# Decay tables of a retention + mixture-of-experts kernel: scans on VectorE in place of a table through DRAM

## The chip, the cores and the metric

The kernel runs on one core of a Trainium2 chip. The metric is the device time of one execution in microseconds (us). The engines are TensorE (PE in the profile, with its weight loads as PEld), VectorE (DVE), ScalarE (ACT), GpSimd (POOL), and SyncE (SP), which issues every DMA of this kernel from one queue.

## The reference

Three layers in a row on 1,536 tokens (2 sequences of 768) with 512 channels. What the change touches is the first, a retention layer with 8 heads of 64 channels and a decay `lam` per head:

```
Dmask   = lam ** (i - j)  for i >= j, else 0        # within a block
lam_pow = lam ** (i + 1)
for each block:
    out   = ((q k^T) * Dmask) v + (q * lam_pow) state
    state = lam ** block * state + (k * lam ** (block - 1 - j))^T v
```

The second layer is a mixture of 4 experts, `out += p[:, e] * (relu(x w1[e]) w2[e])` with `p = probs / (sum(probs) + 1e-9)`. The third is `g = silu(x w_in)`, `out = g w_out`. All data are float32 (the third layer's weights come as 64-bit words).

## The kernel before, in words

The retention layer works in blocks of 128 tokens: 12 units (`u = 2c + b`, block c of sequence b). A unit has four pieces, `prep` (on POOL, from block 1 on: `qs` = q times the query powers `qdec`, and `old` = decayed state), `scores` (on POOL `ks` = k times a column of `dmask`; on PE the products `s`; on DVE `a` = `s * dmask`), `mix` (on PE `xps`, then on ACT and DVE the two halves `xhi`, `xlo` of x) and `carry` (on PE `sps`, the new state). `dmask` holds for each partition and head one row of 128 powers of lam shifted by the partition; `qdec` holds 128 powers for each pair of heads.

Matrix products outside the retention layer split each float32 operand into a high and a low half: ACT makes the high half (L141), and DVE or POOL the low half (L142). Three products of halves replace one. The weights come in pairs of steps: one `u` transfer and one `d` transfer of 512 KB each, into two raw buffers of each kind; the next `u` or `d` is issued when the split of the one before has released its buffer. Weights 0 and 1 of phase "a" are split by DVE, all later ones by POOL.

Phase "a" (the experts) starts with group 0: 8 steps on the 256 tokens of block 0. Step i runs `gemm1(i)` (up, L470, output `ph`, whose high and low half are `hhi` on ACT and `hlo` on DVE, L480 and L481) and `gemm2(i - 2)` (down, L525, output `po`). `gemm1(i)` uses PSUM bank i mod 2, so it waits until `hlo` of step i - 2 has been made. The pieces of the later units are put between the steps: unit 2's `prep` at slot `PREP` (two slots a step), its `scores` after step 3, unit 3's `mix` after step 7. From step 4 on the kernel also loads 64-bit words of the third layer (`words`), halves their scale on ACT (L196) and decodes them on DVE.

The order is written out by hand and is the program's order on each engine: an instruction that waits holds everything behind it on the same engine. That holds for SP's queue too.

`powers()` makes the opening: it loads lam into one row a head, doubles powers by 7 small DVE multiplications, stores the table `zd` to DRAM, and reads it back as `dmask` (512 KB) and `qdec` (256 KB). `gates()` (9 DVE instructions on 12 partitions) normalizes the expert probabilities and stands between the table's making and the first `kv` load. `keep_warm(n)` issues n products of zeros on PE; one keep_warm call of n gives 2n matmul records.

Of the kernel before, what the change touches and what calls it, by code (L numbers as in the profile page):

```python
# [7 lines left out]
F32 = mybir.dt.float32  # L8
# [3 lines left out]
ALU = mybir.AluOpType  # L12
# [3 lines left out]
P = 128  # L16
B, H, S, D = 2, 8, 768, 64
NPAIR = H // 2
# [5 lines left out]
NF = 8  # L24
# [1 line left out]
TW = 512  # L26
HW = DM // 2
FIRST = 6
PREP = 1
NW = E * NF // 2  # L30
NV = NF

# [5 lines left out]
def kernel(  # L38
# [10 lines left out]
    nc = tc.nc  # L49

    def pool(stack, name, bufs=1, side="left", **kw):
        return stack.enter_context(tc.tile_pool(name=name, bufs=bufs, side=side, **kw))
# [10 lines left out]
    dram = pool(ctx, "dram", space=DRAM)  # L63
# [6 lines left out]
    acst = pool(att, "acst", side="right")  # L70
# [1 line left out]
    awk = pool(att, "awk", 2, side="right")  # L72
    w0p = pool(first, "w0p", 2, side="right")

    zd = dram.tile([H, 2 * P], F32, name="zd")
    pd = dram.tile([E, NT // P, P], F32, name="pd")
    wd = [dram.tile([P, 2, 2 * DM], F32, name=f"wd{i}") for i in range(NV)]

    dmask = acst.tile([P, NPAIR, 2, P], F32, name="dmask")
    qdec = acst.tile([P, NPAIR, P], F32, name="qdec")  # L80
    state = [acst.tile([P, NPAIR, D], F32, name=f"state{b}") for b in range(B)]
    zeros = acst.tile([P, NPAIR, P], F32, name="zeros")
# [15 lines left out]
    def load_qk(c, b):  # L98
        t = ald.tile([P, 2, NPAIR, P], F32, tag="qk", name="qkt")
        nc.sync.dma_start(out=t, in_=qk[c, b])  # L100
        qk_t[c, b] = t

    def load_kv(c, b, parts=(slice(0, 2),)):
        if (c, b) not in kv_t:
            kv_t[c, b] = ald.tile([P, 2, H, D], F32, tag="kv", name="kvt")
        for j in parts:
            nc.sync.dma_start(out=kv_t[c, b][:, j], in_=kv[c, b, :, j])
# [25 lines left out]
    def load(j, n=1):  # L133
        for _ in range(n):
            if nxt[j] < len(seq):
                ph, i, src = seq[nxt[j]]
                nxt[j] += 1
                (load_up, load_down)[j](src, i, (ph, i))

    def split(eng, hi, lo, src):  # L140
        nc.scalar.activation(out=hi, in_=src, func=AF.Copy)  # L141
        eng.tensor_tensor(out=lo, in0=src, in1=hi.bitcast(F32), op=ALU.subtract)  # L142
# [13 lines left out]
    def half_up(key, n, eng):  # L156
        hi, lo = up_t[key]
        s = slice(0, 4, 3) if n == 0 else slice(1, 3)
        split(eng, hi[:, s], lo[:, s], raw_t[key, 0][:, s])
        if n:  # L160
            load(0)

    def half_down(key, n, eng):
        hi, lo = down_t[key]
        split(eng, hi[:, n], lo[:, n], raw_t[key, 1][:, n])
        if n:
            load(1)

    def split_half(key, n, eng):

        half_up(key, n, eng)
        half_down(key, n, eng)
# [53 lines left out]
    def flush():  # L226
        while pending:
            pending.pop(0)()
# [21 lines left out]
    def decode_next(more):  # L250

        if jobs[0] < 4 * NV:
# [3 lines left out]
            pending.append(decode(jobs[0]))  # L256
            jobs[0] += 1

    def powers():
        z = acst.tile([H, 2 * P], F32, name="z")  # L260
        nc.sync.dma_start(out=z[:, P:P + 1], in_=lam)
        nc.vector.memset(z[:, :P - 1], 0.0)
        nc.vector.memset(z[:, P - 1:P], 1.0)
        load_probs()
        for b in range(B):
            load_qk(0, b)
        m = 1
        while m < P:
            o = P - 1 + m
            nc.vector.tensor_scalar_mul(z[:, o + 1:o + 1 + m], z[:, P:o + 1], z[:, o:o + 1])  # L270
            m *= 2
        nc.sync.dma_start(out=zd, in_=z)
        gates()
        for b in range(B):
            load_kv(0, b, [1])
        for m in range(2):
            nc.sync.dma_start(
                out=dmask[:, 2 * m:2 * m + 2],
                in_=bass.AP(
                    zd.tensor, zd.offset + m * H * P, [[1, P], [2 * P, NPAIR], [1, P]]  # L280
                ),
            )
        load(0)
        for b in range(B):
            load_kv(0, b, [0])
        for t in range(2):
            nc.sync.dma_start(
                out=qdec[t * D:(t + 1) * D],
                in_=bass.AP(
                    zd.tensor, zd.offset + t * 2 * P + P, [[0, D], [4 * P, NPAIR], [1, P]]  # L290
                ),
            )
        nc.gpsimd.memset(zeros, 0.0)
        keep_warm(3)

    def keep_warm(n):
        warm = psum.tile([P, NPAIR, P], F32, tag="po3", name="warm")
        for _ in range(n):
            nc.tensor.matmul(warm, lhsT=zeros[:, 0], rhs=zeros, start=True, stop=True)  # L299
# [3 lines left out]
    def gate_tile():  # L303
        return const.tile([P, 2 * TW], F32, tag="gate", name="gate", bufs=2)

    def load_probs():
        n = NT // P
        t = gate_tile().rearrange("p (e i) -> p e i", i=P)
        gate_t["probs"] = t[:n, :E], t[:n, E]
        nc.sync.dma_start(out=t[:n, :E], in_=probs)  # L310

    def gates():
        pt, sm = gate_t["probs"]
        nc.vector.tensor_tensor(out=sm, in0=pt[:, 0], in1=pt[:, 1], op=ALU.add)
        nc.vector.tensor_tensor(out=sm, in0=sm, in1=pt[:, 2], op=ALU.add)
        nc.vector.tensor_tensor(out=sm, in0=sm, in1=pt[:, 3], op=ALU.add)
        nc.vector.tensor_scalar_add(sm, sm, 1e-9)
        nc.vector.reciprocal(out=sm, in_=sm)
        for e in range(E):
            nc.vector.tensor_tensor(out=pt[:, e], in0=pt[:, e], in1=sm, op=ALU.mult)  # L320

    def store_gates():
        nc.sync.dma_start(out=pd.rearrange("e r i -> r e i"), in_=gate_t["probs"][0])
# [297 lines left out]
    fill = []  # L621
# [177 lines left out]

    with tc.manual_schedule():  # L800
        powers()
        load(1)
        load(0)
        load(1)
        for i in range(2):
            w_tiles(w0p, ("a", i))
        units = {b: attention(0, b) for b in range(B)}
# [1 line left out]
        def piece(u, j):  # L809
            if u not in units:  # L810
                units[u] = attention(u // B, u % B)
            units[u][j]()
# [2 lines left out]
        piece(1, 0)  # L815
        piece(0, 1)
        piece(1, 1)
        keep_warm(5)
        half_up(("a", 0), 0, nc.vector)
        piece(0, 2)  # L820
        piece(1, 2)
        for b in range(B):
            load_qk(1, b)
        half_up(("a", 0), 1, nc.vector)
        half_down(("a", 0), 0, nc.vector)
        half_down(("a", 0), 1, nc.vector)
        gemm1("a", 0)
        split_half(("a", 1), 0, nc.vector)
        piece(0, 3)
        piece(1, 3)  # L830
# [9 lines left out]
        def attend(slot):  # L840
            skip = FIRST if gi == 0 else 0
            if gi == 0 and slot == PREP:
                piece(2, 0)
# [6 lines left out]
        for i in range(na):  # L850
            gi, f = steps["a"][i]
            if f == 0:
                todo = plan.get(gi, [])
                if gi == 2:
                    first.close()
                elif gi == E:
                    flush()
                    store_decoded()
                    att.close()
                    tmp["comb"] = pool(ctx, "comb")  # L860
                    tmp["sums"] = pool(early, "sums", side="right")
                    mixing = combine(*x_raw)
            if i:
                gemm1("a", i)
            attend(2 * f)
            flush()
            if 2 <= i < na - 1:
                gemm2("a", i - 2)
            attend(2 * f + 1)
            if i == 3:  # L870
                store_gates()
            elif i == 5:
                load_gate("a", 0)
            elif i in (8, 18, 25):
                load_gate("a", {8: 1, 18: 2, 25: 3}[i])
            elif i == na - 4:
                load_gate("c", 0)
            if i == PREP + 3:
                start_decoder()
            elif PREP + 3 < i < 4 * NF and (i % 2 and i != 15 or i in (6, 10, 16, 18, 20)):  # L880
                decode_next(i < 4 * NF - 3)

            if i == 0:
                split_half(("a", 1), 1, nc.vector)
            elif i in (1, 3):
                w_tiles(wp, ("a", (i + 3) // 2))
                split_half(("a", (i + 3) // 2), 0, nc.gpsimd)
            elif i in (2, 4):
                split_half(("a", (i + 2) // 2), 1, nc.gpsimd)
            elif i >= 13 and i % 2:  # L890
                if i < na - 3:
                    split_up(("a", (i - 5) // 2))
                elif i == na - 3:
                    left_sums(("c", 0))
                else:
                    left_second(("c", 0))
                if 15 <= i < na - 1:
                    split_down(("a", (i - 7) // 2))
            elif i == na - 2:
                left_first(("c", 0))  # L900
            if gi == E:
                for job in mixing[f * 11 // NF:(f + 1) * 11 // NF]:
                    job()
# [131 lines left out]
```

## Time and profile before

| | |
|---|---|
| device time, median of 3 runs | 816.72 us (816.11 to 817.9) |
| profiled execution, span from first to last instruction | 814.1 us |
| median less that span | 2.6 us |
| PE busy | 807.5 us (99%) |
| DVE, ACT, POOL busy | 529.7, 326.4, 453.4 us (65%, 40%, 56%) |
| bytes moved | 95.93 MB, 118 GB/s on average |

The profiled execution's own time is given by its span; what lies around it is the difference to the median. Busy shares are averages over the whole span, and PE's record of being busy includes products of zeros and the pipelined ends of matmuls. So a change in the first 20 us can't be read from these shares; it is read from the order of time in the opening.

### The profile page before, as it was taken

To read this page: it belongs to the slowest core of one execution; us is meant where nothing else is said; L and a number is where in the kernel's file an instruction comes from. 1 tells how busy PE (TensorE), PEld (TensorE's weight loads), DVE (VectorE), ACT (ScalarE), POOL (GpSimd) and SP (SyncE) were. 2 spreads that over 40 slices of the span, in tenths; PEclk is the share of its full clock that TensorE was granted. 3 is DMA by queue.
4 is the path that set the end of the run, shared out by engine and by line. 5 is a ranking of instruction groups with operands and counts; after the bars stand their busy time and mean duration, and the time that the engine had idled before them with its cause. 6 is when DMAs were issued, how large, how long until landed. Compare 5 with 4: busy or idle time off the path is not lost.

```text
span 814.1 us, 11017 instructions
## 1 busy us (share of the span) xinstructions
PE 807.5 (99%) x4224; PEld 666.9 (82%) x4224; DVE 529.7 (65%) x762; ACT 326.4 (40%) x528; POOL 453.4 (56%) x333
## 2 busy tenths in 40 slices
PE   9999999999999999999999999999999999999998
PEld 5899877778888888888888888888888888888886
DVE  6375797545668588878888878865454345666666
ACT  3433332433446333333333333334454465444431
POOL 1824755525666666666666666754346666555631
PEclk9999999999999999999999999999999999999999
DMA  8885767533324223223322211122233131111002
GB/s 296 317 321 195 250 240 240 189 102 117 104 104 142 90 91 115 94 83 98 112 94 85 94 61 70 46 90 90 78 103 105 52 103 52 52 52 52 27 1 103
DMA packets 31434, 95.93 MB, mean 118 GB/s; under 512 B 3409, under 2 KB 5001, under 8 KB 31381
## 3 DMA queue, kind: packets, MB, share of 16 engines
q1 hardware_dynamic: 31380, 95.23, 35.1%
q8 instruction: 33, 0.54, 0.3%
q14 instruction: 21, 0.16, 0.1%
HBM read 83.65 MB, written 11.57 MB: 117 GB/s over the span
## 4 chain that ended last, share of the span: by engine, by line
PE 93%; DVE 3%; DMA 2%; issue 1%; ACT 1%; POOL 0%; SPq 0%; ACTq 0%; POOLq 0%
PE po L707 32%; PE po L525 14%; PE ph L470 14%; PE y L647 12%; PE x L647 8%; PE z L647 8%; PE warm L299 1%; PE s L374 1%; PE xps L401 1%; DMA words<-wts 1%; DMA u<-wts 1%; DVE dec L213 1%; DVE dec L209 1%; DVE tail L206 1%; PE xps L397 1%
## 5 line engine op out<-in xcount | busy, mean ns | idle before, releaser
L707 PE MATMUL po<-hlo,dh 128*128 128x512 f32 x384 | 149.6, 390 | 0.0
L707 PE MATMUL po<-hhi,dh 128*128 128x512 f32 x384 | 149.6, 390 | 0.0
L707 PE MATMUL po<-hhi,dl 128*128 128x512 f32 x384 | 149.6, 389 | 0.0
L719 DVE TENSOR_TENSOR acc<-po,acc 128x512 f32<-128x512 f32 x176 | 117.2, 683 | 43.2 <-PE po L707 43.2
L142 POOL TENSOR_TENSOR ub<-u,ua 128x256 fp32r<-128x256 f32 (+2 forms) x48 | 74.8, 1559 | 107.4 <-ACT ua L141 103.1
L142 POOL TENSOR_TENSOR dl<-d,dh 128x1024 fp32r<-128x1024 f32 (+1 forms) x48 | 114.3, 2380 | 28.8 <-ACT dh L141 28.8
L664 POOL TENSOR_TENSOR s<-s,s 128x512 f32<-128x512 f32 x48 | 63.2, 1319 | 50.3 <-ACT s L659 50.2
L142 POOL TENSOR_TENSOR uc<-u,uc 128x512 fp32r<-128x512 f32 x24 | 31.2, 1301 | 96.7 <-ACT uc L141 96.7
L707 PEld LDWEIGHTS po<-hhi,dl 128*128 128x128 f32 x384 | 72.1, 188 | 15.0
L707 PEld LDWEIGHTS po<-hhi,dh 128*128 128x128 f32 x384 | 72.1, 188 | 14.9
L707 PEld LDWEIGHTS po<-hlo,dh 128*128 128x128 f32 x384 | 72.1, 188 | 14.9
L497 ACT ACTIVATE hhi<-ph 128x512 fp32r<-128x512 f32 x40 | 23.9, 599 | 97.0 <-DVE ph L491 83.3
L142 POOL TENSOR_TENSOR ub<-us,ua 128x1024 fp32r<-128x1024 f32 x24 | 58.4, 2433 | 5.3 <-ACT ua L141 5.3
L525 PE MATMUL po<-hhi,dh 128*128 128x512 f32 (+1 forms) x224 | 58.7, 364 | 0.0
L525 PE MATMUL po<-hhi,dl 128*128 128x512 f32 (+1 forms) x224 | 57.7, 360 | 0.0
L525 PE MATMUL po<-hlo,dh 128*128 128x512 f32 (+1 forms) x224 | 57.6, 359 | 0.0
L470 PE MATMUL ph<-xhi,ua 128*128 128x512 f32 (+1 forms) x224 | 55.6, 371 | 1.2 <-DVE hlo L481 0.7
L141 ACT ACTIVATE dh<-d 128x1024 fp32r<-128x1024 f32 (+1 forms) x52 | 51.3, 988 | 9.2 <-POOL ub L142 2.6
L470 PE MATMUL ph<-xhi,ub 128*128 128x512 f32 (+1 forms) x224 | 53.1, 359 | 0.0
L470 PE MATMUL ph<-xlo,ua 128*128 128x512 f32 (+1 forms) x224 | 53.1, 359 | 0.0
L498 DVE TENSOR_TENSOR hlo<-ph,hhi 128x512 fp32r<-128x512 f32 x40 | 27.7, 692 | 27.8 <-ACT hhi L497 27.8
L470 PEld LDWEIGHTS ph<-xhi,ua 128*128 128x128 f32 x224 | 37.9, 189 | 9.4 <-DVE hlo L481 0.9
(128 smaller groups left out, 1577.7 us busy)
## 6 DMA issues: line engine op xcount, KB each, us to landing
u<-wts SPq DMA_DIRECT2D x32, 512.0 KB, 3.6
d<-wts SPq DMA_DIRECT2D x32, 512.0 KB, 3.7
words<-wts SPq DMA_DIRECT2D x32, 512.0 KB, 5.1
wd<-dec SPq DMA_DIRECT2D x32, 256.0 KB, 3.1
u<-wd SPq DMA_DIRECT2D x16, 512.0 KB, 3.7
d<-wd SPq DMA_DIRECT2D x16, 512.0 KB, 3.7
qkt<-qk SPq DMA_DIRECT2D x12, 512.0 KB, 5.9
kvt<-kv SPq DMA_DIRECT2D x10, 512.0 KB, 5.6
```

The costliest lines, as they stand in the source:

```text
L141: nc.scalar.activation(out=hi, in_=src, func=AF.Copy)
L142: eng.tensor_tensor(out=lo, in0=src, in1=hi.bitcast(F32), op=ALU.subtract)
L206: nc.vector.tensor_scalar(out=tail, in0=low, scalar1=2.0 ** -29, scalar2=None, op0=ALU.mult)
L209: nc.vector.scalar_tensor_tensor(out=f, in0=high, scalar=3, in1=f, op0=ALU.logical_shift_left, op1=ALU.bitwise_or,)
L470: nc.tensor.matmul(pt[:, :n], lhsT=w, rhs=x[:, k, o:o + n], start=(j == 0), stop=(j == len(ops) - 1),)
L497: nc.scalar.activation(out=hi, in_=pt, func=AF.Copy)
L498: nc.vector.tensor_tensor(out=lo, in0=pt, in1=hi.bitcast(F32), op=ALU.subtract)
L525: nc.tensor.matmul(po_t[d][:, :n], lhsT=w[:, d * P:(d + 1) * P], rhs=h[:, :n], start=(begin and j == 0), stop=(last and j == 2),)
L647: nc.tensor.matmul(to, lhsT=a[:, k * P:(k + 1) * P], rhs=b[:, k], start=(first and j == 0), stop=(j == len(ops) - 1), skip_group_check=not ...
L664: nc.gpsimd.tensor_tensor(out=t, in0=a, in1=b, op=ALU.add)
L707: nc.tensor.matmul(po, lhsT=w, rhs=h, start=(j == 0), stop=(j == len(ops) - 1))
L719: nc.vector.tensor_tensor(out=a, in0=po, in1=a, op=ALU.add)
```

## The change

`dmask` and `qdec` are made in place. lam is read twice from DRAM: as `lamall`, all 8 values on each of 128 partitions, and as `lamhalf`, 4 values on each partition (even heads on the lower 64, odd heads on the upper 64). On POOL an `affine_select` writes `unit`, a 128x128 tile with ones on an antidiagonal. On DVE 8 scans (`state = lam * state + unit`) write the rows of `dmask`, and 4 scans from 1.0 write `qdec`. The table `zd`, its store and its four reads go.

The opening's transfers are in a new order: lamall, q and k of sequence 0, v of sequence 0, q and k of sequence 1, v of sequence 1, the first `u` and `d`, the two lamhalf reads, both k-by-head halves, the second `u`, the probabilities; the second `d` comes after `mix` of unit 1. `gemm1(0)` stands ahead of the split of the first `d`. `mix` of unit 0 stands ahead of the first split of `u`. `keep_warm(3)` and `keep_warm(5)` become one `keep_warm(2)`. The query powers are made after step 1 (`query_powers`), the gates after step 2, and unit 2's `prep` moves from slot 1 to slot 5.

```
-PREP = 1
+PREP = 5
+DECODE = 4
...
+    def lam_scan(out, lam_col, add, initial):
+
+        nc.vector.tensor_tensor_scan(
+            out=out,
+            data0=lam_col.to_broadcast([P, P]),
+            data1=add,
+            initial=initial,
+            op0=ALU.mult,
+            op1=ALU.add,
+        )
+
     def powers():
-        z = acst.tile([H, 2 * P], F32, name="z")
-        nc.sync.dma_start(out=z[:, P:P + 1], in_=lam)
...
-        load_probs()
-        for b in range(B):
-            load_qk(0, b)
-        m = 1
-        while m < P:
-            o = P - 1 + m
-            nc.vector.tensor_scalar_mul(z[:, o + 1:o + 1 + m], z[:, P:o + 1], z[:, o:o + 1])
-            m *= 2
-        nc.sync.dma_start(out=zd, in_=z)
-        gates()
-        for b in range(B):
-            load_kv(0, b, [1])
-        for m in range(2):
-            nc.sync.dma_start(
-                out=dmask[:, 2 * m:2 * m + 2],
...
+        nc.sync.dma_start(
+            out=lam_t["all"], in_=bass.AP(lam.tensor, lam.offset, [[0, P], [1, H]])
+        )
+        nc.gpsimd.memset(zeros, 0.0)
+        unit_t = acst.tile([P, P], F32, name="unit")
+        nc.gpsimd.affine_select(
+            out=unit_t,
+            in_=zeros[:, 0],
...
+        keep_warm(2)
+        load_qk(0, 0)
+        load_kv(0, 0, [1])
+        load_qk(0, 1)
+        load_kv(0, 1, [1])
         load(0)
-        for b in range(B):
-            load_kv(0, b, [0])
+        load(1)
         for t in range(2):
             nc.sync.dma_start(
-                out=qdec[t * D:(t + 1) * D],
...
+                out=lam_t["half"][t * D:(t + 1) * D],
+                in_=bass.AP(lam.tensor, lam.offset + t, [[0, D], [2, NPAIR]]),
             )
-        nc.gpsimd.memset(zeros, 0.0)
-        keep_warm(3)
+        for h in range(H):
+            lam_scan(dmask[:, h // 2, h % 2], lam_t["all"][:, h:h + 1], unit_t, 0.0)
+
+    def query_powers():
+        for p in range(NPAIR):
+            lam_scan(qdec[:, p], lam_t["half"][:, p:p + 1], zeros[:, 0], 1.0)
...
         powers()
-        load(1)
+        for b in range(B):
+            load_kv(0, b, [0])
         load(0)
-        load(1)
+        load_probs()
...
         piece(1, 1)
-        keep_warm(5)
+        piece(0, 2)
         half_up(("a", 0), 0, nc.vector)
-        piece(0, 2)
         piece(1, 2)
+        load(1)
         for b in range(B):
             load_qk(1, b)
         half_up(("a", 0), 1, nc.vector)
+        gemm1("a", 0)
         half_down(("a", 0), 0, nc.vector)
         half_down(("a", 0), 1, nc.vector)
-        gemm1("a", 0)
...
-            if i == 3:
+            if i == 1:
+                query_powers()
+            elif i == 2:
+                gates()
+            elif i == 3:
                 store_gates()
```

## Rows read from the trace of the kernel before

**Rows 1.** The page: span, and the chain that ended last by engine.

```profile
span 814.1 us, 11017 instructions
...
PE 93%; DVE 3%; DMA 2%; issue 1%; ACT 1%; POOL 0%; SPq 0%; ACTq 0%; POOLq 0%
```

**Rows 2.** Waits of PE from 60 us to the end: total, times, longest.

```profile
PE sps L426 <- ACT xraw L412: 0.2, 1, 0.2
```

**Rows 3.** Timeline, PE, opening: start, us, instruction, idle before and its releaser.

```profile
1.31 5.49 PE L299 MATMUL warm<-zeros 128*128 128x512 f32 x6 [1.31 <-POOL zeros L293]
6.73 2.07 PE L374 MATMUL s<-qkt 64*128 64x128 f32 x32
8.73 4.56 PE L299 MATMUL warm<-zeros 128*128 128x512 f32 x10
13.22 1.97 PE L401 MATMUL xps<-a,kvt 128*64 128x128 f32 x32
15.67 0.78 PE L470 MATMUL ph<-xhi,ua 128*128 128x256 f32 x4 [0.48 <-ACT xhi L415]
...
17.33 1.15 PE L426 MATMUL sps<-kvt,ks 128*64 128x64 f32 x32
18.41 0.75 PE L470 MATMUL ph<-xhi,ua 128*128 128x256 f32 x4
...
23.73 0.74 PE L470 MATMUL ph<-xhi,ua 128*128 128x256 f32 x4 [0.74 <-DVE hlo L481]
```

**Rows 4.** Timeline, DVE and POOL, opening: start, us, instruction, idle before.

```profile
0.73 0.52 POOL L293 MEMSET zeros<- 128x512 f32 x1 [0.29 <-POOLq L1022]
...
2.09 1.76 DVE L270 TENSOR_SCALAR z<-z 8x1 f32<-8x1 f32 x7 [1.10 <-DMA z<-lam]
...
4.96 0.94 DVE L318 RECIPROCAL gate<-gate 12x128 f32<-12x128 f32 x1
...
5.93 0.88 DVE L320 TENSOR_TENSOR gate<-gate 12x128 f32<-12x128 f32 x4
...
10.42 2.74 DVE L382 TENSOR_TENSOR a<-s,dmask 128x256 f32<-128x256 f32 x8 [3.61 <-DMA dmask<-zd]
...
13.51 2.40 POOL L360 TENSOR_TENSOR ks<-kvt,dmask 128x512 f32<-128x512 f32 x2 [12.26 <-DMA kvt<-kv]
```

**Rows 5.** Windows: stretch, busy PE, PEld, DVE, ACT, POOL, clock, DMA share, GB/s.

```profile
0.00:5.00 5.00, 3.69 (x5) 1.63 (x6) 2.73 (x14) 1.28 (x1) 0.73 (x5) 1.00 0.46 157
5.00:10.00 5.00, 5.00 (x38) 2.78 (x37) 1.78 (x5) 0.00 (x0) 0.00 (x0) 1.00 0.78 266
...
20.00:25.00 5.00, 4.26 (x35) 4.05 (x35) 3.67 (x6) 1.55 (x4) 2.33 (x2) 1.00 1.03 410
...
32.00:35.00 3.00, 3.00 (x41) 2.63 (x38) 1.23 (x4) 2.07 (x6) 3.00 (x4) 1.00 0.81 195
```

**Rows 6.** Timeline, all engines: from the third u transfer to unit 3's mix.

```profile
17.16 0.33 SPq L115 DMA_DIRECT2D u<-wts  x1
...
20.46 1.30 POOL L344 TENSOR_TENSOR qs<-qkt,qdec 128x512 f32<-128x512 f32 x1 [4.55 <-DMA qkt<-qk]
...
21.71 1.08 POOL L348 TENSOR_TENSOR old<-state,qdec 128x256 f32<-128x256 f32 x1
...
24.52 0.63 ACT L141 ACTIVATE ua<-u 128x512 fp32r<-128x512 f32 x1 [3.45 <-DMA u<-wts]
...
29.00 1.30 POOL L142 TENSOR_TENSOR dl<-d,dh 128x512 fp32r<-128x512 f32 x1
...
31.61 0.96 SPq L233 DMA_DIRECT2D words<-wts  x2
...
39.97 0.69 ACT L196 ACTIVATE words<-words 128x512 f32<-128x512 f32 x1 [4.66 <-DMA words<-wts]
...
42.63 0.66 PE L397 MATMUL xps<-qs,state 64*64 64x128 f32 x14 [0.17 <-DVE a L382]
```

**Rows 7.** Tile qkt up to 60 us: its transfers, from issue to landing.

```profile
DMA to landing us min/median/max: 3.7/6.3/9.8
```

More of the change, by code (lines that the diff above doesn't have):

```diff
@@ L73 @@
     w0p = pool(first, "w0p", 2, side="right")
-    zd = dram.tile([H, 2 * P], F32, name="zd")
     pd = dram.tile([E, NT // P, P], F32, name="pd")
@@ L257, in decode_next @@
             jobs[0] += 1
-    def powers():
-        z = acst.tile([H, 2 * P], F32, name="z")
-        nc.sync.dma_start(out=z[:, P:P + 1], in_=lam)
-        nc.vector.memset(z[:, :P - 1], 0.0)
-        nc.vector.memset(z[:, P - 1:P], 1.0)
-        load_probs()
-        for b in range(B):
-            load_qk(0, b)
-        m = 1
-        while m < P:
-            o = P - 1 + m
-            nc.vector.tensor_scalar_mul(z[:, o + 1:o + 1 + m], z[:, P:o + 1], z[:, o:o + 1])
-            m *= 2
-        nc.sync.dma_start(out=zd, in_=z)
-        gates()
-        for b in range(B):
-            load_kv(0, b, [1])
-        for m in range(2):
-            nc.sync.dma_start(
-                out=dmask[:, 2 * m:2 * m + 2],
[L279 to L282, printed above, removed]
+    lam_t = {}
@@ new lines, in lam_scan @@
+    def lam_scan(out, lam_col, add, initial):
[7 more added lines that the diff above has]
+        )
+    def powers():
+        lam_t["all"] = acst.tile([P, H], F32, name="lamall")
+        lam_t["half"] = acst.tile([P, NPAIR], F32, name="lamhalf")
+        nc.sync.dma_start(
[6 more added lines that the diff above has]
+            in_=zeros[:, 0],
+            pattern=[[1, P]],
+            base=1 - P,
+            channel_multiplier=1,
+            compare_op=ALU.not_equal,
+            fill=1.0,
+        )
+        keep_warm(2)
[3 more added lines that the diff above has]
+        load_kv(0, 1, [1])
@@ L283, in powers @@
         load(0)
-        for b in range(B):
-            load_kv(0, b, [0])
+        load(1)
         for t in range(2):
             nc.sync.dma_start(
-                out=qdec[t * D:(t + 1) * D],
-                in_=bass.AP(
-                    zd.tensor, zd.offset + t * 2 * P + P, [[0, D], [4 * P, NPAIR], [1, P]]
-                ),
-            )
-        nc.gpsimd.memset(zeros, 0.0)
-        keep_warm(3)
+                out=lam_t["half"][t * D:(t + 1) * D],
+                in_=bass.AP(lam.tensor, lam.offset + t, [[0, D], [2, NPAIR]]),
+            )
@@ L877 @@
                 load_gate("c", 0)
-            if i == PREP + 3:
+            if i == DECODE:
                 start_decoder()
-            elif PREP + 3 < i < 4 * NF and (i % 2 and i != 15 or i in (6, 10, 16, 18, 20)):
+            elif DECODE < i < 4 * NF and (i % 2 and i != 15 or i in (6, 10, 16, 18, 20)):
                 decode_next(i < 4 * NF - 3)
```

## The prediction

> **What bounds the kernel now.** I read the page first: the chain that ended last lies on PE for 93% of the span of 814.1 us [rows 1]. Then the waits of PE: from 60 us on PE waited 0.2 us in all [rows 2]. So PE's stream is dense from there to the end, and the change can give or take time only by making that dense stream begin earlier or later. All that counts is in the first 45 us, so I read those in order of time.
>
> In the opening PE issues products of zeros, 16 records of them, and real work of only about 4 us, until `gemm1(0)` starts at 15.67 us [rows 3]. What is late there is the mask: DVE stands idle for 3.61 us until `dmask` lands at 10.42 [rows 4], which has gone from lam to a table, to DRAM, and back. The windows say what this costs the transfers: the DMA engines are 46% busy in the first 5 us and 78% in the next 5, then full (1.03, at 410 GB/s in 20 to 25 us) [rows 5]. About 3.8 us of DMA time is lost (0.54 x 5 + 0.22 x 5), because SP's queue stood behind the table.
>
> The last tight place is at 42.63: unit 3's `mix` waits 0.17 us for `a` [rows 6]. Behind it is a chain through many engines. The third `u` lands at 24.52; ACT and POOL split this weight pair until 30.30 (29.00 + 1.30); this frees the raw buffers, SP issues the fifth `u` and `d` and then, at 31.61, the first `words`; these land at 39.97, and ACT, which is in order, has been waiting for them for 4.66 us with `hhi` of step 6 behind. `hlo`, `a` and `mix` follow [rows 6]. So there are two paths to the dense stream, PE's own and that of `words`, and before they arrive within 0.2 us of each other. The gain is the smaller of what the two paths gain.
>
> **Transfers.** The first big one is issued near 1.2 us (engines start at 0.73 [rows 4], one issue takes 0.48, half of the 0.96 for two [rows 6]). The quickest load of q and k took 3.7 us to land [rows 7], so 4.9. From there the queue never runs dry. At 410 GB/s [rows 5] 512 KB (524,288 bytes) take 1.28 us and half of it 0.64: v of sequence 0 at 5.5, q and k of sequence 1 at 6.8, its v at 7.5, the first `u` at 8.7, the first `d` at 10.0. The two lamhalf reads are 512 pieces of 4 bytes, which no row shows. Between nothing and the price of two 512 KB transfers, 2.6 us, I take 0.7, nearer to the lower end, since they carry only 2 KB. Then the k halves at 11.4 and 12.0, the second `u` at 13.3, the second `d` at 14.6, block 1's q and k at 17.2, the third `u` at 18.5.
>
> **Mask.** The single lamall read should land as the lam read did, by 2.1 to 2.6 [rows 4]. `affine_select` follows the memset (done at 1.25); it costs between nothing and POOL's 1.30 us for a pass four times as wide [rows 6], so it is done by 2.6 and hidden behind lamall. A scan over 128 columns stands in no row. The lower bound is 0.22 us (a 12x128 product, 0.88 for four), the upper 0.94 (the reciprocal, DVE's dearest row of 128 columns); I take 0.34, the 128x256 product (2.74 for eight) [rows 4], for a scan's element must wait for the one before it. Eight are 2.7 us: `dmask` is there at 5.3, with 4.4 and 10.1 as bounds.
>
> [...]
>
> **PE's own path.** One unit's `scores` take 1.03 us and its `xps` 0.98 (halves of 2.07 and 1.97) [rows 3], four mask products 1.37. Unit 0: `scores` 4.9 to 6.0, `a` to 7.4. Unit 1: `scores` 6.8 to 7.9, `a` to 9.3. `xps` of unit 0 from 7.9 to 8.9, of unit 1 from 9.4 to 10.4; ACT's `xhi` some 0.8 later. `gemm1(0)` at 11.2 against 15.67; its weights (8.7, and two splits of 0.7) are there. The zeros of keep_warm(2) end before 4.9 (4 of the 6 records that now take 5.49). Now the k halves, which move behind more transfers, are late: `ks` takes 1.2 us a unit [rows 4] from 11.4, so 13.8, and the two `carry` pieces stand in PE's order ahead of `gemm1(1)`: 14.5 against 18.41. From there to `gemm1(3)` PE now takes 5.32 us, of which 0.74 is a wait for `hlo` behind DVE's splits [rows 3]. With `gemm1(0)` ahead of the splits, and no POOL work beside them, I find that `hlo` ready at 18.9 in DVE's order, so `gemm1(3)` at 19.1 against 23.73. PE's path gains 4.6 us.
>
> **The words path.** The third `u` is issued once the first is split, near 12.4 (two splits behind unit 1's `a`), and lands at 18.5 by bytes; the same transfer now needs 7.3 us behind a full queue (17.16 to 24.52 [rows 6]), which would be 19.7. I take 19.1; the upper bound is 21.3, if the split is done only at 14. From there to the `words` issue it now takes 7.09 us (24.52 to 31.61). Unit 2's `prep` comes on top. Now POOL does it before the third `u` is there (20.46 to 22.79), for nothing; in slot 5 it stands between the two halves of this split, and its 1.30 + 1.08 = 2.38 us count in full [rows 6]. `words` at 19.1 + 7.09 + 2.38 = 28.57 against 31.61: 3.0 us. If they land as slowly as now, `mix` of unit 3 moves by 3.0.
>
> **Moved at no cost.** The gates (2.96 us, from the table's end at 3.85 to 6.81 [rows 4]) go to DVE after step 2, about 20.6 to 23.6. Behind them wait `hlo` of step 3, wanted by `gemm1(5)` near 28, and `a` of unit 2, wanted by its `mix` near 26: done by 25.3, so 0.8 us to spare. The query powers, 4 x 0.34 = 1.4 us, delay `hlo` of step 2 to 20.6, wanted at 23.5. Without that cover they would cost 3.0 and 1.4, but on PE's path, which has 1.6 us more than the words path. The probabilities (24 KB) and their store stay ahead of their use. The removed `zd` traffic (0.77 MB, 1.9 us at 410 GB/s) is already in the list of landings.
>
> **Sum.** The smaller gain decides: 3.0 us. Span 814.1 - 3.0 = 811.1; the median lies 2.6 us above that span, so 816.7 - 3.0 = 813.7 us. A measurement here tells about 0.2% (1.6 us) from no change.
>
> **Rivals.**
> *PE's path alone decides* (15%). In 32 to 35 us the DMA engines moved only 195 GB/s at a share of 0.81 [rows 5], less than half of the 410 of other stretches. If `words` then come about 2 us sooner after their issue, the words path gains 5 and PE's 4.6 rules: 812.1. Against it: nothing in the change touches that stretch.
> *The supply eats it: no change* (19%). The third `u` lands at 21.3, or POOL is slowed by DVE's scans and gates beside its splits; each us there takes one off. At 21.3 the gain is 31.61 - 30.77 = 0.8: 815.9. Scans of 0.94 lead to the same place: `dmask` at 10.1 is as late as the table was (10.42), and the change would not do what it says. For it: the DMA engines are full in 20 to 25 us as it is [rows 5], and unit 2's `prep` is a new charge on POOL.
> *PE runs at its low clock: slower* (9%). [...]
>
> [...]
>
> **Chances.** The forecast 57% (812.6 to 815.0), PE's path alone 15%, no change 19%, slower 9%. Faster by over 0.2% (below 815.1): 0.72; within: 0.19; slower: 0.09. The range for 8 in 10 takes in PE's path alone and the no-change case to its end: 811.9 to 816.6.
>
> **What would show it.** `a` of unit 0 starts near 6 instead of 10.42, after eight scans of about 0.34 us. `gemm1(0)` starts near 11.2, then PE waits for `ks`; `gemm1(1)` at 14.5, `gemm1(3)` at 19.1 without a wait for `hlo`. `qs` of unit 2 stands between two splits. `words` are issued near 28.6, and `mix` of unit 3 waits some 1.7 us for `a`, the difference of the two paths. PE's waits from 60 us on stay near 0.2. The prediction is wrong if `dmask` comes after 9, if records of one shape are spaced twofold beyond 10 us, or if `words` move by another amount than PE's stream at 45 us.

## The result: slower by 0.8%

The changed kernel takes 823.12 us (median of 4 runs, 821.26 to 824.51), the kernel before beside it 816.41 us (815.83 to 817.9): a ratio of 1.0077, 95% interval 1.0058 to 1.0095. The forecast was 813.7 with a range of 811.9 to 816.6. The span of the profiled execution grows from 814.1 [rows 1] to 821.7 us. PE waits for nothing from 60 us on (0.2 us in all before [rows 2]), so the loss lies in the first 60 us.

PE's timeline of the changed kernel (start, us, instruction, idle before and its releaser), to be read against [rows 3, 6]:

```profile
5.43 1.16 PE L386 MATMUL s<-qkt 64*128 64x128 f32 x16 [0.39 <-DMA qkt<-qk]
7.80 1.68 PE L386 MATMUL s<-qkt 64*128 64x128 f32 x16 [1.21 <-DMA qkt<-qk]
...
12.96 0.78 PE L482 MATMUL ph<-xhi,ua 128*128 128x256 f32 x4 [0.49 <-ACT xhi L427]
...
17.31 0.69 PE L438 MATMUL sps<-kvt,ks 128*64 128x64 f32 x16 [2.63 <-POOL ks L372]
18.77 1.12 PE L438 MATMUL sps<-kvt,ks 128*64 128x64 f32 x16 [0.78 <-POOL ks L372]
19.82 1.22 PE L482 MATMUL ph<-xhi,ua 128*128 128x256 f32 x4
...
25.12 0.63 PE L482 MATMUL ph<-xhi,ua 128*128 128x256 f32 x4
...
30.66 0.62 PE L537 MATMUL po<-hhi,dh 128*128 128x256 f32 x4
...
36.70 1.63 PE L409 MATMUL xps<-qs,state 64*64 64x128 f32 x16 [4.51 <-DVE a L394]
38.26 1.98 PE L413 MATMUL xps<-a,kvt 128*64 128x128 f32 x16
40.16 1.22 PE L482 MATMUL ph<-xhi,ua 128*128 128x256 f32 x4
...
42.78 0.69 PE L438 MATMUL sps<-kvt,ks 128*64 128x64 f32 x16
```

`gemm1(0)` does start earlier (12.96 against 15.67). Then PE waits 2.63 and 0.78 us for `ks`, and `gemm1(1)`, at 19.82, is already 1.4 us later than before. The great loss is at 36.70: `mix` of unit 2 waits 4.51 us for `a`, and the products behind it run at about half the rate (`xps` 3.46 us instead of 1.62).

DVE's timeline of the changed kernel shows, in its first rows, the scans and the `a` of unit 0, and then what the `a` of unit 2 waits behind (its own start is the last row):

```profile
3.65 2.63 DVE L263 TENSOR_TENSOR_SCAN dmask<-lamall,unit 128x128 f32<-128x128 f32 x8 [3.65 <-DMA lamall<-lam]
6.63 1.42 DVE L394 TENSOR_TENSOR a<-s,dmask 128x256 f32<-128x256 f32 x4 [0.35 <-PE s L386]
...
26.67 0.88 DVE L326 TENSOR_TENSOR gate<-gate 12x128 f32<-12x128 f32 x1
27.58 1.25 DVE L327 TENSOR_TENSOR gate<-gate 12x128 f32<-12x128 f32 x1
28.86 0.59 DVE L328 TENSOR_TENSOR gate<-gate 12x128 f32<-12x128 f32 x1
29.49 1.20 DVE L329 TENSOR_SCALAR gate<-gate 12x128 f32<-12x128 f32 x1
30.73 0.94 DVE L330 RECIPROCAL gate<-gate 12x128 f32<-12x128 f32 x1
31.71 3.91 DVE L332 TENSOR_TENSOR gate<-gate 12x128 f32<-12x128 f32 x4
35.55 0.41 DVE L493 SCALAR_TENSOR_TENSOR hlo<-ph,hhi 128x256 fp32r<-128x256 f32 x1
35.88 1.27 DVE L394 TENSOR_TENSOR a<-s,dmask 128x512 f32<-128x512 f32 x2
```

The nine gate instructions run from 26.67 to 35.62: 8.95 us, where they took 2.96 in the opening [rows 4]. Four products that took 0.88 take 3.91. The reciprocal keeps its 0.94, and `hlo` and `a`, which have one of their operands in PSUM, take 0.41 and 1.27 (0.42 and 1.28 in the kernel before). POOL works from 24.84 us to past the end of the gates without a pause (splits of weights, `qs`, `old`, `ks`).

Windows of the changed kernel (columns as in [rows 5]): the DMA engines, full from 5 to 10 us (share 1.02), fall to 0.21 from 10.5 to 14 us; and from 36 to 40 us the granted clock is 0.50.

```profile
10.50:14.00 3.50, 3.01 (x34) 2.77 (x31) 2.55 (x8) 2.27 (x6) 0.00 (x0) 0.83 0.21 64
36.00:40.00 4.00, 3.30 (x32) 2.58 (x32) 1.48 (x3) 0.00 (x0) 1.33 (x2) 0.50 0.94 342
```

SP was not late: lamhalf's two reads were issued from 4.33 us on, and the k halves, the second `u`, the probabilities and the second `d` were all issued behind them before the hole begins. What stood next in the queue is lamhalf. SP's row, and the time that the tile's view gives the two reads to land:

```profile
4.33 1.39 SPq L297 DMA_DIRECT2D lamhalf<-lam  x2
...
DMA to landing us min/median/max: 7.7/8.9/10.0
```

POOL's timeline has the first k half behind them, at 15.89 where the forecast had 11.4:

```profile
15.89 2.82 POOL L372 TENSOR_TENSOR ks<-kvt,dmask 128x512 f32<-128x512 f32 x2 [14.27 <-DMA kvt<-kv]
```

The same places of PE's timeline in the kernel before:

```profile
29.42 0.64 PE L525 MATMUL po<-hhi,dh 128*128 128x256 f32 x4
...
30.95 0.67 PE L397 MATMUL xps<-qs,state 64*64 64x128 f32 x16
...
32.57 0.75 PE L470 MATMUL ph<-xhi,ua 128*128 128x256 f32 x4
...
34.20 0.69 PE L426 MATMUL sps<-kvt,ks 128*64 128x64 f32 x16
```

Worked out along PE's order: `gemm2(2)` stands 1.24 us later than before (30.66 against 29.42 at its start); the wait adds 4.51; `xps` of unit 2 takes 3.46 instead of 1.62 us (36.70 to 40.16, against 30.95 to 32.57), 1.84 more; `gemm1(5)` 2.62 instead of 1.63, 0.99 more. That is 8.58 us at the `carry` of unit 2 (42.78 against 34.20). About 0.6 comes back at `mix` of unit 3, which no longer waits, and some 0.4 in small pieces after it, whose place was not followed: 7.6 in the span.

### The profile page after: what moved, and what is told of

Same layout as the page of the kernel before. It is cut to its first block, busy times and chain, and to the rows that moved or that the text cites. A ratio compares the mean times of both kernels' runs of the same rounds, so it can differ in the third digit from the quotient of the medians.

```text
span 821.7 us, 10996 instructions
## 1 busy us (share of the span) xinstructions
PE 806.4 (98%) x4212; PEld 668.6 (81%) x4212; DVE 527.5 (64%) x765; ACT 326.3 (40%) x528; POOL 459.5 (56%) x334
## 4 chain that ended last, share of the span: by engine, by line
PE 96%; DMA 2%; DVE 2%; ACT 0%; SPq 0%; issue 0%
PE po L719 32%; PE ph L482 16%; PE po L537 16%; PE y L659 12%; PE x L659 8%; PE z L659 8%; PE xps L413 2%; PE s L386 1%; DMA d<-wts 1%; PE xps L409 1%; DMA qkt<-qk 1%; PE sps L438 1%; DVE gate L332 0%; DVE dl L142 0%; DVE gate L327 0%; DVE gate L329 0%
## 5 line engine op out<-in xcount | busy, mean ns | idle before, releaser
L676 POOL TENSOR_TENSOR s<-s,s 128x512 f32<-128x512 f32 x48 | 68.9, 1437 | 44.7 <-ACT s L671 44.6
```

The lines of the kernel that those rows point to most:

```text
L676: nc.gpsimd.tensor_tensor(out=t, in0=a, in1=b, op=ALU.add)
```

## The experiments

Theory A: two things went wrong that the prediction had priced too low, the gates beside POOL's work and the 4-byte reads; the low clock follows from the waits. Theory B: the low clock of PE, for want of products of zeros, is the cause by itself. Theory C: the gates are hidden behind other work and cost nothing. Each ratio is to the kernel before, run beside it.

**Gates back in the opening** (between the mask products and `mix` of unit 0, probabilities loaded first):

```
-        load_probs()                     # behind the second u
+        load_probs()                     # behind lamall
...
         piece(1, 1)
+        gates()
         piece(0, 2)
...
-            elif i == 2:
-                gates()
```

> The changed kernel, with the probabilities loaded behind lamall and the gates made on DVE between the mask products of unit 1 and the mix of unit 0, where POOL stands idle. Theory A (gates in step 2 take 8.9 us because POOL's splits hold them up, and hold the mask product of unit 2): the gates take about 3.0 us, mix of unit 2 no longer waits 4.5 us, and the 2.8 us that its xps and the gemm1 behind it lose at the low clock come back: about 6 us less than the changed kernel's 823.1, near 817. Theory B (the low clock for want of products of zeros is the cause by itself): the gates get quick but xps and gemm1 of 36 to 42 us stay spaced twofold, and no more than 3 to 4 us come back, near 819.5. Theory C (the gates are hidden): no change, 823.

817.96 us, ratio 1.0020 (1.0010 to 1.0029). The gates take 3.04 us there (10.71 to 13.75), `mix` of unit 2 waits for nothing, and its products run at the rate of the kernel before (32.91 to 34.53, 1.62 us). 5.2 us came back. C falls. B falls as the cause at 36 us: no products of zeros were added, and the low clock there is gone with the wait (granted clock 1.00 from 30 to 40 us). The opening still has one: behind waits of 1.68 and 0.78 us for `ks`, `gemm1` of steps 1 and 2 takes 4.47 us (20.03 to 24.50) against 2.98 before, at a granted clock of 0.66 from 20 to 25 us.

**lamhalf copied on DVE from lamall:**

```
-        for t in range(2):
-            nc.sync.dma_start(out=lam_t["half"][t * D:(t + 1) * D], ...)
...
     def query_powers():
+        for t in range(2):
+            r = slice(t * D, (t + 1) * D)
+            nc.vector.tensor_copy(lam_t["half"][r],
+                lam_t["all"].rearrange("p (j t) -> p j t", t=2)[r, :, t])
```

> The changed kernel without the two lamhalf reads: lamhalf is copied on DVE from lamall, two copies of 64x4 ahead of the query powers. Theory A (1,024 bytes in pieces of 4 bytes stop the DMA engines for some 4 us at 10 to 14 us, so that the k halves land at 15.8): the k halves land near 11.5, gemm1 of step 1 starts near 15 to 16 instead of 19.8, the DMA share of 10 to 15 us rises from 0.38 to about 1.0, and the time falls by 3.5 to 4.5 us, near 819, the wait of mix of unit 2 for the gates staying near 4.5 us. Rival (the engines run dry because SP issues late, behind waits of its own): the share of 10 to 15 us stays low and the time within 1 us of 823.

819.07 us, ratio 1.0032 (1.0023 to 1.0042): 4.1 less. The DMA share of 10 to 15 us is 1.03 (0.38 in the changed kernel):

```profile
10.00:15.00 5.00, 4.14 (x56) 3.41 (x56) 4.04 (x10) 3.42 (x9) 2.53 (x2) 1.00 1.03 398
```

PE's timeline is near the predicted one: `gemm1` of step 0 at 12.17, of step 1 at 15.31, of step 3 at 19.66 (forecast 11.2, 14.5, 19.1). The wait for `a` stays, 6.1 us. So the 4-byte reads were most of the difference between the forecast opening and the measured one: at `gemm1` of step 3, 5.5 us of 6.0 (25.12 against 19.66 and 19.1).

**Both:**

> Both edits together. Theory A: the two causes add up, 10 us less than the changed kernel, near 813 to 814.5, below the kernel before (816.4); what is left is the words path, with mix of unit 3 waiting 1 to 2 us. Theory B (clock): PE's clock still falls in the gaps of the opening and the time stays at 816 or above.

818.01 us, ratio 1.0013 (1.0000 to 1.0027): a miss. With the k halves early, POOL makes `ks` at 12.50, and there the gates' four products meet it. DVE's timeline:

```profile
12.68 2.49 DVE L333 TENSOR_TENSOR gate<-gate 12x128 f32<-12x128 f32 x4
15.10 0.74 DVE L429 TENSOR_TENSOR xlo<-xps,xhi 128x256 fp32r<-128x256 f32 x2
```

2.49 us instead of 0.88, the same loss in another place. `xlo` and the first splits come later, `gemm1(0)` waits 3.84 us for `xlo`, and the third `u` is issued at 17.72 (13.75 with the copies alone).

**Gates in step 2, their sum in PSUM:**

```
         pt, sm = gate_t["probs"]
+        sm = bank([P, TW], "sm")[:NT // P, :P]
```

> The changed kernel with the gates in step 2 as they are, but their running sum in a PSUM bank, so that eight of the nine instructions have at most one operand in SBUF besides their output. If what holds them up beside POOL is two SBUF operands on DVE (the mask products and hlo, which read PSUM, keep their 0.64 and 0.42 us in the same stretch), the gates take 3 to 4 us instead of 8.9 and the time falls as in the first kernel, near 817 to 818. If POOL's splits hold up anything on DVE that writes or reads SBUF there, they stay near 8 us and the time near 823.

820.27 us, ratio 1.0044 (1.0030 to 1.0059). In the same place, with POOL splitting from 25.16 us on without a pause, the first gate, whose two operands both lie in SBUF, takes 0.86 us, and the sums and products with the running sum in PSUM 0.29 and 0.87, what they take beside an idle POOL (0.28 and 0.89 in the first experiment). DVE's timeline:

```profile
27.01 0.86 DVE L327 TENSOR_TENSOR sm<-gate 12x128 f32<-12x128 f32 x1
27.91 0.29 DVE L328 TENSOR_TENSOR sm<-sm,gate 12x128 f32<-12x128 f32 x1
28.23 0.29 DVE L329 TENSOR_TENSOR sm<-sm,gate 12x128 f32<-12x128 f32 x1
28.55 0.29 DVE L330 TENSOR_SCALAR sm<-sm 12x128 f32<-12x128 f32 x1
28.87 0.95 DVE L331 RECIPROCAL sm<-sm 12x128 f32<-12x128 f32 x1
29.86 0.87 DVE L333 TENSOR_TENSOR gate<-gate,sm 12x128 f32<-12x128 f32 x4
```

3.72 us in all against 8.95. The time fell less than expected, because the sum holds a PSUM bank that `scores` of unit 2 wants: PE waits 3.1 us for the gates.

**Gates on POOL in the opening, with the copies:**

```
-        nc.vector.tensor_tensor(out=sm, in0=pt[:, 0], in1=pt[:, 1], op=ALU.add)
+        nc.gpsimd.tensor_tensor(out=sm, in0=pt[:, 0], in1=pt[:, 1], op=ALU.add)
...
+        gates()                  # behind the scans; 1e-9 and reciprocal on DVE
```

The other sums and the four products move to POOL in the same way.

> The changed kernel with lamhalf copied on DVE, and the gates in the opening: the probabilities loaded behind lamall, the sums and the four products of the gates on POOL (idle from 1.6 us until ks), the reciprocal and the constant on DVE behind the scans. Theory A (only the gates beside POOL's splits and the 4-byte reads went wrong): the opening is that of the kernel with the copies (gemm1 of step 3 at 19.7), mix of unit 2 does not wait for a, words are issued near 29.3 and mix of unit 3 then waits 1 to 2 us: 813.5 to 814.5, faster than the kernel before by 2 to 3 us. Theory B (the low clock): PE's clock falls in the opening and the time stays at 816 or above.

814.96 us, ratio 0.9985 (0.9974 to 0.9996): faster than the kernel before by 1.2 us, within the range of the forecast, but 0.5 above what was expected here. Its ten executions spread from 813.05 to 816.54 us; the two with a mean granted clock of 1.000 took 813.05 and 813.69, the two with 0.995 took 815.88 (the profiled one) and 816.54, and the six between took 814.27 to 816.47. `words` are issued at 30.48, and the words path of the prediction now binds. PE's timeline around `mix` of unit 3:

```profile
40.98 0.43 PE L411 MATMUL xps<-qs,state 64*64 64x128 f32 x2 [2.03 <-DVE a L396]
41.58 0.80 PE L411 MATMUL xps<-qs,state 64*64 64x128 f32 x14 [0.17 <-DVE a L396]
42.31 1.97 PE L415 MATMUL xps<-a,kvt 128*64 128x128 f32 x16
44.22 1.22 PE L539 MATMUL po<-hhi,dh 128*128 128x256 f32 x4
```

The wait was forecast at 1.7 us and is 2.03; ACT has stood 6.76 us waiting for `words` before it. Not forecast: from 40 to 45 us the granted clock is 0.70 on average, and the 16 products of `xps` at 42.31 take 1.97 us instead of 1.09, so that in this execution PE is at 44.22 where the kernel before was at 44.25.

**The kernel before with the gates after step 2, and nothing else:**

```
         nc.sync.dma_start(out=zd, in_=z)
-        gates()
...
-            if i == 3:
+            if i == 2:
+                gates()
+            elif i == 3:
```

> One part of the change alone: the kernel before, with the gates after step 2 in place of the opening. Theory A: POOL splits weights there from 25.2 us on, the gates start near 28.4 (behind hlo of step 2) and take about 8 us, a of unit 2 comes near 37 instead of 28.4, its mix waits 5 us or more, and PE loses 2 to 3 us more at the low clock: 822 to 825. Theory C (the gates are hidden, the clock's loss comes from the opening): 816 to 817.

824.42 us, ratio 1.0098 (1.0079 to 1.0116). This one move costs 8.3 us by itself. In this trace 1.4 us of it stand before the gates begin (`gemm1` of step 3 at 25.14 against 23.73): the first `d` landed 7.2 us after its issue instead of 6.0, and why was not followed. DVE's timeline (first and last of the gates), then PE's:

```profile
27.98 0.87 DVE L313 TENSOR_TENSOR gate<-gate 12x128 f32<-12x128 f32 x1
...
33.45 3.45 DVE L319 TENSOR_TENSOR gate<-gate 12x128 f32<-12x128 f32 x4
```

```profile
37.88 1.72 PE L396 MATMUL xps<-qs,state 64*64 64x128 f32 x16 [5.45 <-DVE a L381]
39.53 1.97 PE L400 MATMUL xps<-a,kvt 128*64 128x128 f32 x16
```

**The kernel before with the two lamhalf reads, into a tile that nothing reads:**

```
         load(0)
+        half = acst.tile([P, NPAIR], F32, name="lamhalf")
+        for t in range(2):
+            nc.sync.dma_start(out=half[t * D:(t + 1) * D], ...)
         for b in range(B):
             load_kv(0, b, [0])
```

> One part of the change alone: the kernel before, with the two lamhalf reads issued behind the first u, into a tile that nothing reads. Theory A: the DMA engines run dry for some 4 us, the k halves land 3 to 4 us later than at 13.4 to 14.2, ks and the carries follow, and the time rises by 2 to 4 us, to 818.5 to 820.5. Rival (512 pieces of 4 bytes cost no more than the 0.7 us of the prediction): under 1 us, 816.3 to 817.2.

820.52 us, ratio 1.0047 (1.0029 to 1.0064): 2,048 bytes that nobody uses (two reads of 1,024 each; an expectation above counts one) cost 4.4 us. The window of 12 to 15 us:

```profile
12.00:15.00 3.00, 2.93 (x35) 1.92 (x33) 2.31 (x7) 1.31 (x4) 0.00 (x0) 1.00 0.05 0
```

No byte moves for 3 us, and the DMA engines do not count as busy either (0.05).

**The changed kernel with zeros in PE's waits:**

```
+        keep_warm(3)
         piece(0, 3)
+        keep_warm(1)
         piece(1, 3)
...
+            if u == 2:                      # ahead of xps
+                for _ in range(10):
+                    nc.tensor.matmul(po_t[0][:, :CW], lhsT=zeros[:, 0],
+                        rhs=zeros[:, :2], start=False, stop=False, ...)
```

> The changed kernel with products of zeros in PE's waits: four calls ahead of the carries (about 3.4 us of records) and ten of 256 columns ahead of mix of unit 2 (about 4.3 us, added as zeros to the sums of gemm2). The waits stay. [...] If the clock is not raised by products of zeros, or the waits take back what it gives, 822 to 823.

821.54 us, ratio 1.0060 (1.0044 to 1.0077). In the profile the low clock is gone where the zeros stand: `xps` of unit 2 takes 2.12 us (35.76 to 37.88) instead of 3.46, `gemm1` of step 1 1.52 instead of 2.47, and from 34 to 40 us the granted clock is 1.00. The time is 1.6 us lower, and the interval overlaps that of the changed kernel. So in the trace the low clock had a price of its own, 1.34 and 0.95 us in these two places, a part of the loss; in the time it is not clear of noise.

**Later decoding of words, on top of the gates on POOL and the copies:**

```
-  (i % 2 and i != 15 or i in (6, 10, 16, 18, 20))
+  (i % 2 and i not in (5, 15) or i in (8, 10, 16, 18, 20, 22))
```

> The kernel with the copies and the gates in the opening, and the first two decodings of words in steps 7 and 8 instead of 5 and 6 (one more in step 22, so that as many are made in phase a). If ACT waiting for words is what mix of unit 3 waits for (2.0 us there, and 1.6 more at the low clock behind it), that wait goes, PE's own path rules, and mix of unit 3 starts near 38.6 to 39 instead of 42.6 in the kernel before: 3.5 to 4 us below the kernel before, near 812.3. Rival (something else is late next, such as qs or the fifth u): 814 to 815, no better than with the early words.

> The same with one call of zeros on PE between the scores of units 0 and 1. If the clock falls in the opening for the gap of 1.5 us there, scores and xps of unit 1 come back to 1.16 and 1.1 us, gemm1 of step 0 starts 1 us earlier, and the time falls by up to 1 us more, near 811.5. If q and k of sequence 1 or DVE's order hold gemm1 of step 3 anyway, no change beside the kernel without zeros.

> Control: the kernel before with the later decodings alone. There mix of unit 3 waited 0.17 us for a, so no more than 0.2 us is to be had: 816.0 to 816.5, no change. If the words path held more than that wait shows, below 815.3.

The first: 813.34 us, ratio 0.9964 (0.9950 to 0.9977). The wait at `mix` of unit 3 is gone. PE's timeline:

```profile
37.89 0.67 PE L411 MATMUL xps<-qs,state 64*64 64x128 f32 x16
38.49 1.09 PE L415 MATMUL xps<-a,kvt 128*64 128x128 f32 x16
```

37.89 against 42.04 before, where the first records of the same products stood ahead of the wait in [rows 6]: in this execution, of 811.77 us, PE's path gained 4.2 us there (forecast 4.6, at `gemm1` of step 3). A part goes to a new wait of 0.9 us of `gemm2` for DVE's sums (`acc`). With zeros between the `scores`: 812.44 us, ratio 0.9953 (0.9941 to 0.9966). `gemm1` of step 0 started at 12.80 there and not earlier than the 12.27 without, so the expected mechanism did not show, and the two intervals overlap. But the profiled execution without zeros is one of the two in six in which the clock hardly fell (811.71 and 811.77 us at 1.000 and 0.999; the other four took 812.95 to 814.19 at 0.996 to 0.998), and with zeros all five took 812.34 to 812.76 at 0.999 to 1.000. So what the zeros changed is the spread. Where the clock falls without them, the profile of the gates on POOL shows, whose opening is the same: its granted clock is 0.78 from 5 to 10 us and 0.88 from 10 to 15, and `gemm1` of step 0 starts at 13.27. The control, later decoding in the kernel before: 816.62 us, ratio 1.0006 (0.9997 to 1.0014), no change. The later decoding is worth nothing until PE's path has been made shorter.

**lamhalf from whole rows of 32 bytes, in the same place of the queue:**

```
-                in_=bass.AP(lam.tensor, lam.offset + t, [[0, D], [2, NPAIR]]),
+                in_=bass.AP(lam.tensor, lam.offset, [[0, D], [1, H]]),   # then two DVE copies
```

> The changed kernel with the two lamhalf reads in the same place of the queue, but as 64 whole rows of 32 bytes each (all 8 values), the wanted 4 picked by copies on DVE. 128 pieces of 32 bytes in place of 512 of 4. If the small, strided pieces stop the DMA engines, most of the gap at 10.5 to 14.5 us goes and the time is near that of the kernel with copies alone (819.1), 818.5 to 820. If any read of lam to all partitions from this place in the queue stops them, the gap stays and the time is 822 to 824.

820.52 us, ratio 1.0048 (1.0031 to 1.0065). The DMA share of 10 to 15 us is 0.93 (the last column but one; clock ahead of it) where the changed kernel had 0.38, so the hole is gone, and `gemm1` of step 1 starts at 16.58 instead of 19.82:

```profile
10.00:15.00 5.00, 0.90 0.93 356
```

The time is 1.4 us above that of the copies; the intervals overlap. It is the way these reads are cut into 4-byte pieces that stops the engines, not reading lam there. That it is the count of pieces alone is ruled out by the kernel before, whose `qdec` reads were 512 pieces too, of 512 bytes. Whether the size or the step of 8 bytes between pieces does it was not tried.

## Why the prediction was wrong, point by point

**What bounds the kernel, and the two paths: right in kind, too large in size.** With the gates and the 4-byte reads both out of the way the kernel took 814.96 us, and both paths showed: PE's stream came earlier (`gemm1` of step 3 at 20.71, and at 19.78 with the later decoding; forecast 19.1, 23.73 before), and the `words` path held `mix` of unit 3 back, by a wait of 2.03 us for `a`. But `words` were issued at 30.48 (29.27 with the later decoding), 1.1 to 2.3 us earlier than before and not 3.0. The third `u` was already late, issued at 15.16 (13.88) where the forecast had 12.4. With the `words` path moved out of the way it was 813.34 us; that this is near the forecast 813.7 is chance, since the forecast had that path in place.

**The step that failed, and cost most: "Moved at no cost".** The gates were priced at 2.96 us, from rows in which POOL stood idle [rows 4], and moved into a stretch that the same prediction filled with POOL's splits back to back. There they took 8.95. That is 6.0 us more, against a cover of 0.8 us ahead of `a`. Shown by the gates moved alone (+8.3 us), moved back (-5.2), and with their sum in PSUM (3.72 us in the same place). The trace of before held the warning. On DVE the split of the second half of the second `u` took 1.25 us at 21.07, where that of the first half had taken 0.68; POOL stood idle beside the first and ran `qs` and `old` beside the second [rows 6]:

```profile
18.71 0.68 DVE L142 TENSOR_TENSOR ub<-u,ua 128x512 fp32r<-128x512 f32 x1
...
21.07 1.25 DVE L142 TENSOR_TENSOR ub<-u,ua 128x512 fp32r<-128x512 f32 x1
```

The no-change rival looked at this meeting of DVE and POOL from the wrong side: it feared for POOL, whose splits kept their 1.3 us.

The traces show which instructions it cost. Beside POOL instructions of 1.3 us the sums and products with both inputs in SBUF took 0.3 to 1.0 us longer than in the opening (0.88, 1.25 and 0.59 instead of 0.27 to 0.28 for the sums, 0.98 instead of 0.22 for one product), those with one in PSUM did not (0.29 and 0.22). The constant, with its one input in SBUF, took 1.20 instead of 0.21, and 0.29 with it in PSUM; why, no trace shows. Priced by the 0.57 us that the second split above took longer than the first (1.25 less 0.68), the three sums, the constant and the four products would have come to 4.6 us more than in the opening, an estimate from these two rows; measured were 6.0. The prediction left the two rows out.

**The term that was mis-sized: lamhalf.** 0.7 us, bounded above by 2.6, measured at about 4: 3.5 us of DMA engines at a share of 0.21 in the changed kernel, 4.4 us of time in the kernel before, 4.1 us back without the reads. The bound failed because it reasoned from bytes and no row had reads cut like this, and with it failed "From there the queue never runs dry". The k halves, the `carry` pieces and all that stands behind them in PE's order moved by it.

**The low clock: a rival that came true in part.** In the opening of the changed kernel the granted clock did fall, to 0.50 from 9 to 11 us, and that was hidden behind the wait for `ks`, 2.63 us. What it cost on the path, 0.93 us at `gemm1(1)` and 1.84 + 0.99 behind `mix` of unit 2, came after waits that the two faults had made. Removing the gates from step 2 removed it at 36 us (granted clock 1.00 from 30 to 40 us), without any zeros. With both faults out it was no longer hidden: of two profiles with the same opening, the one with a mean granted clock of 0.995 (0.78 from 5 to 10 us, 0.88 from 10 to 15) has `gemm1(0)` at 13.27 and the one with 0.999 has it at 12.27. The executions of these two kernels spread by 3.5 and 2.5 us, those with one call of zeros in the opening by 0.4.

**Scans and `affine_select`: right; PE's opening: 1.0 us late without the 4-byte reads (`gemm1(0)` at 12.17, forecast 11.2).** Eight scans took 2.63 us (forecast 2.7). One took 0.33 us for 128 columns, near the 0.34 of the product of 256 columns that it was priced by (2.74 for eight [rows 4]). `affine_select` took 0.29 us. lamall landed at 3.65 and not by 2.6, which put `a` at 6.63 instead of near 6.

## What to carry to other kernels

A duration belongs to the stretch it was measured in: before an instruction is moved on VectorE, look at what GpSimd does in its new place (here the gates took 2.96 us beside an idle GpSimd and 8.95 beside its splits). If both its inputs are in SBUF, price it by what such instructions take beside GpSimd in a trace of the kernel, or put one operand in PSUM where a bank is free (here 3.72 us in place of 8.95). Reads cut into 4-byte pieces are to be judged by their pieces and not by their bytes (here about 4 us for 2,048 bytes); two copies on VectorE, 0.33 us together, took their place. And a wait on TensorE can cost more than itself: behind waits of 4.51 and 2.03 us products here ran at half the rate (`xps` of unit 2 took 3.46 us instead of 1.62 behind the first, 16 products of unit 3's `xps` 1.97 instead of 1.09 behind the second).

## What the runs showed of the hardware that was not expected

Two reads of 1,024 bytes each, cut into 4-byte pieces, left the 16 DMA engines at a share of 0.05 from 12 to 15 us in the kernel before, and at 0.21 from 10.5 to 14 us in the changed kernel, with ordinary transfers queued behind them.

With the gates on POOL, PE's granted clock was 1.00 from 35 to 40 us and 0.70 from 40 to 45. A wait of 2.03 us ended at 40.98, and from about 42 us on the products ran at half the rate: 16 of `xps` took 1.97 us instead of 1.09. A wait of that length did not always do it: in the kernel before with the lamhalf reads, the products behind a wait of 2.07 us kept their rate (0.73 us for four, and a granted clock of 1.00 until 30 us).

```profile
23.66 0.73 PE L476 MATMUL ph<-xhi,ua 128*128 128x256 f32 x4 [2.07 <-ACT ua L141]
```

In the changed kernel the granted-clock column showed 0.50 where the rate was halved (36 to 40 us); in the opening of the kernel before it had read 1.00 while the first six records of zeros were spaced by 0.85 us and the later ten by 0.43 [rows 3, 5].
